# Luna attention and a gated MLP on one core: an earlier load of v2, first scores ahead of the first packed block, and a changed order of fills

## The chip, the cores and the metric

The kernel runs on one core of a Trainium2 chip. The metric is the device time in microseconds of one execution. Before the change the median of 8 runs is 254.1 us (253.71 to 257.84). Instructions are named by engine: PE is TensorE (PEld its weight loads), DVE is VectorE, ACT is ScalarE, POOL is GpSimd, and SP is the queue of SyncE, which only issues DMAs here.

## The reference

```python
def sm_attn(qq, kk, vv):
    s = scale * np.matmul(qq, kk.transpose(0, 1, 3, 2))
    a = softmax(s)                        # max subtracted, sum + 1e-9
    return np.matmul(a, vv)

p_packed = sm_attn(p, k, v)               # p: 32 packed queries a head
out = sm_attn(q, p_packed, p_packed)      # q: 576 queries a head
x = out.transpose(0, 2, 1, 3).reshape(B * S, H * D)
h = x @ w_in                              # 4608 x 512 by 512 x 2048
return (h * np.cos(h)) @ w_out            # 2048 x 512
```

B = 8 batches, H = 8 heads, S = 576 positions, D = 64. The inputs are float32; the kernel computes in bfloat16 with float32 sums.

## The kernel before

The eight batches run one after the other as a software pipeline whose order is written out by hand: each engine executes its own instructions in program order and waits on semaphores for the others.

For one batch b the stages are:

- `load(n, b)` issues on POOL a DMA that casts k, q or v of the batch to bfloat16 (tiles kbf with two buffers, qbf and vbf with one). `permute_v(b)` copies vbf to vp so that heads lie beside each other: 2.75 us on POOL for all batches but the first.
- k and q are transposed, either by TensorE and copies (`pe_T`, batches 0 and 1) or by a DMA issued on SP (`xbar`, from batch 2 on). SP also issues all output DMAs, in program order with these.
- `s1(b)`: scores of the 32 packed queries against k (16 small matmuls, in two halves y, into two PSUM buffers psA), then two exponentials on ACT (tile a1). `recips(b)` makes 1/sum (r1, and rs1 scaled) on DVE from the sums.
- a1 is transposed to a1T by TensorE (`a1_pe`, `a1_one`) or by a DMA on SP (`a1_xbar`).
- `pp(b)`: the packed block, 24 matmuls of vp and a1T; the result is copied to ppT by DVE and ACT.
- `ppw(b, n)`: the packed block times a quarter n of w_in, evacuated to PPW. x is never formed: h is a2n times PPW.
- `s2(b)`: scores of the 576 queries against the packed keys, exponentials (a2u) on ACT. `sums2(b, y)` sums them by a matmul with ones and takes the logarithm on ACT; `normalise(b)` takes two exponentials on ACT and two products on DVE (a2n).
- `h_mm(b, fc)`, fc from 0 to 15: four matmuls give 128 rows of h in a psA buffer, ACT takes the sine with a shift (cosT), DVE multiplies it by the same buffer (gT) and so frees it.
- The output of batch b, 16 matmuls for each chunk of 128 rows, isn't a stage of its own: `fill(n)` issues the next n of these matmuls of the previous batch, and is put where TensorE would wait. A finished chunk is copied to osb by DVE or ACT in turn and sent off by SP. Batch 0 is filled from the end of its own h loop on. The rows 512 to 575 of two batches are joined in one chunk (`joint`, copied by POOL).

`slot(s, hooks, keep, heavy)` runs the 16 steps of h_mm with the fills that are left spread over the steps by weight 1 + heavy[fc]. A hook (fc, f) runs f after step fc; where fc is in heavy, half of the step's fills go ahead of it.

PSUM: pool A has three buffers psA of two banks, taken in turn by everything but the output and the calls with own=True, which take the two banks of pool O.

The change touches `s1` (L133), `a1_one` (L164), the start (L382 to L396), the stretch between batch 0's h loop and slot 1 (L432 to L450), the weights of slots 1 and 2 (L449, L483), and the fills of the loop over batches 3 to 7 (L496, L512). A copy of one element to `gate` on POOL (L444, L479, L504) makes everything behind it on POOL, loads above all, wait until the tile it reads has arrived.

Of the kernel before, what the change touches and what calls it, by code (L numbers as in the profile page):

```python
# [15 lines left out]
def kernel(  # L16
# [55 lines left out]
    def copy(eng, out, in_):  # L72
        if eng is ACT:
            ACT.copy(out=out, in_=in_)  # L74
        else:
            eng.tensor_copy(out=out, in_=in_)  # L76
# [4 lines left out]
    def load(n, b):  # L81
        bf[n, b] = bf_pool.tile([TP, H, C * D], BF16, name=n + "bf", tag=n + "bf", bufs=2 if n == "k" else 1)
        G.dma_start(out=bf[n, b], in_=srcs[n][b].rearrange("h (p c) d -> p h (c d)", c=C))

    def permute_v(b, eng=G):
        vp[b] = vp_pool.tile([TP, C, H * D], BF16, name="vp", tag="vp")
        copy(eng, vp[b].rearrange("p c (h d) -> p c h d", h=H),
             bf["v", b].rearrange("p h (c d) -> p c h d", c=C))
# [5 lines left out]
    def pe_T(n, b, engs=(V, V, V), groups=(0, 1, 2), own=False):  # L94
        if 0 in groups:
            xT[n, b] = att_pool.tile([128, H * 3, TP], BF16, name=n + "T", tag=n + "T", bufs=2 if n == "k" else 1)
        t = xT[n, b]
        flat = bf[n, b].rearrange("p h x -> p (h x)")
        for i in groups:
            ps = bank(BF16) if own else psa(BF16)[:, 0, :]  # L100
            for j in range(8):
                o = 8 * i + j
                nc.tensor.transpose(ps[:, j * TP:(j + 1) * TP], flat[:, o * 128:(o + 1) * 128],  # L103
                                    ident[0:TP, 0:TP])
            copy(engs[i], t[:, 8 * i:8 * i + 8].rearrange("p a x -> p (a x)"),
                 ps[:, 0:8 * TP])

    def bank(dt=FP32):
        return O.tile([128, 512 if dt == FP32 else 1024], dt, name="ot", tag="ot")

    def pack_p(b0, b1, flat=None):
        ng = 2 * (b1 - b0)
        if flat is None:
            flat = psa(BF16).rearrange("p a x -> p (a x)")
        for g in range(ng):
            nc.tensor.transpose(flat[:, g * 128:(g + 1) * 128],
                                p_bf[:, 2 * b0 + g].rearrange("p t d -> p (t d)"), ident)
        V.tensor_copy(out=P2[:, b0:b1].rearrange("p b h n -> p (b h n)"), in_=flat[:, 0:ng * 128])
# [11 lines left out]
            ps.append(t)  # L130
        return ps

    def s1(b):  # L133
        ps = scores(P2[:, b], xT["k", b])
        sm = small.tile([128, 2], FP32, name="sums1")
        for y in range(2):
            ACT.activation(  # L137
                out=a1[b % 2][:, y, :, 0:TP].rearrange("p (e m) x -> p e m x", e=2),
                in_=ps[y][:, :, 0:HS].rearrange("p e (m x) -> p e m x", m=3),
                func=AF.Exp, scale=scale, accum_out=sm[:, y:y + 1])  # L140
        sums1[b] = sm

    def recips(b):
        r1[b] = small.tile([128, 2], FP32, name="r1")
# [19 lines left out]
    def a1_one(b):  # L164
        t = a1T[b] = att_pool.tile([128, 2, C, 128], BF16, name="a1T", tag="a1T")
        ps = psa(BF16)
        for y in range(2):
            for c in range(C):
                nc.tensor.transpose(ps[0:TP, y, c * 128:(c + 1) * 128], a1[b % 2][:, y, c, 0:TP], ident)
            copy(V, t[0:TP, y].rearrange("p c x -> p (c x)"), ps[0:TP, y, 0:C * 128])  # L170

    def pp(b, own=False, engs=(V, ACT)):
# [16 lines left out]
    def ppw(b, n, eng=None, own=False, later=False, cuts=((0, 512),)):  # L189
        if b not in PPW:  # L190
            PPW[b] = ppw_pool.tile([128, 2, DF], BF16, name="PPW", tag="PPW")
        two = isinstance(eng, tuple)
        if own:
            ps = [bank(), bank()]
        else:
            t = psa()
            ps = [t[:, 0, :], t[:, 1, :]]
        for x in range(4):
            for y in range(2):
                r = slice(64 * y, 64 * y + 64)  # L200
                nc.tensor.matmul(ps[y][32 * x:32 * x + 32, :], ppT[b % 2][r, 2 * x + y, :],  # L201
                                 w_in_bf[r, x, n * 512:(n + 1) * 512], start=True, stop=True)

        def evacuate(cuts=cuts):
            if own or two:
                for a, z in cuts:
                    for y in range(2):
                        copy(eng[y] if two else eng, PPW[b][:, y, n * 512 + a:n * 512 + z], ps[y][:, a:z])
            else:
                copy(eng or (V, ACT)[n % 2], PPW[b][:, :, n * 512:(n + 1) * 512], t)  # L210
        if later:
            return [lambda c=c: evacuate((c,)) for c in cuts]
        evacuate()
# [8 lines left out]
    def sums2(b, y):  # L222
        if b not in lns:
            lns[b] = att_pool.tile([128, 2, S], FP32, name="lns", tag="lns")
        ps = psa()
        for e in range(2):
            nc.tensor.matmul(ps[:, e, 0:HS], ones_blk, a2u[b][:, y, e * HS:(e + 1) * HS],  # L227
                             start=True, stop=True)
        ACT.activation(out=lns[b][:, y].rearrange("p (e x) -> p e x", e=2),  # L229
                       in_=ps[:, :, 0:HS], func=AF.Ln)  # L230

    def normalise(b):
        a2n[b] = a2n_pool.tile([128, 2, S], BF16, name="a2n", tag="a2n")
        for y in range(2):
            ACT.activation(out=lns[b][:, y], in_=lns[b][:, y], func=AF.Exp, scale=-1.0)  # L235
        for y in range(2):
            V.scalar_tensor_tensor(out=a2n[b][:, y], in0=a2u[b][:, y], scalar=r1[b][:, y:y + 1],  # L237
                                   in1=lns[b][:, y], op0=ALU.mult, op1=ALU.mult)
# [81 lines left out]
    def fill(n):  # L320
        while n > 0 and filler[1] > 0:
            next(filler[0])
            filler[1] -= 1
            n -= 1
# [13 lines left out]
    def warm(n):  # L338
        wps = bank()
        for _ in range(n):  # L340
            nc.tensor.matmul(wps, wz[:, 0:128], wz, start=True, stop=True)  # L341
# [40 lines left out]
    dup_p(2, 4, V)  # L382
    sums2(0, 0)
    sums2(0, 1)
    pe_T("k", 1, (V, V, V))
    pack_p(1, 2, bank(BF16))
    warm(2)
    cut_ppw, rest_ppw = ppw(0, 0, V, own=True, later=True, cuts=((0, 128), (128, 512)))
    normalise(0)
    cut_ppw()  # L390
    s1(1)
    a1_one(1)
    rest_ppw()
    recips(1)
    load("k", 2)
    permute_v(1)  # L396
    for fc in range(NFC):
        h_mm(0, fc)()
        if fc in (1, 5, 8):
            ppw(0, 1 + fc // 4, (ACT, V), own=True)  # L400
        if fc == 10:
            pp(1, own=True, engs=(ACT, ACT))
        if fc in (11, 12, 13):
            pe_T("q", 1, (V, ACT, V), (fc - 11,), own=True)
        if fc == 13:
            set_filler(0)
        if fc >= 14:
            fill(2)
# [15 lines left out]
    def pw2(b, n=0, eng=None):  # L424
        ppw(b, n, eng)
        ppw(b, n + 1, eng)

    def tk(n, b, i):
# [1 line left out]

    ACT.preload_act_table_set(EXP_SET)
    s2(1)  # L432
    ppw(1, 0, V)
    load("q", 2)
    load("k", 3)
    load("v", 2)
    dup_p(4, 2 * B, G)
    fill(8)
    sums2(1, 0)
    sums2(1, 1)  # L440
    xbar("k", 2)
    xbar("q", 2)
    xbar("k", 3)
    G.tensor_copy(out=gate, in_=xT["k", 3][0:1, 0, 0:1])  # L444
    load("q", 3)
    ppw(1, 1, V)
    normalise(1)
    fill(14)
    slot(1, [(3, lambda: pw2(1, 2, (ACT, V))), (6, lambda: pack_p(2, 5)), (8, lambda: pack_p(5, B)),  # L449
             (8, lambda: (permute_v(2), load("v", 3), load("k", 4)))], 4)  # L450

    fill(1000)
    set_filler(1)
# [26 lines left out]
    for n, b in (("v", 4), ("q", 4), ("k", 5)):  # L480
        load(n, b)
    fill(8)
    slot(2, [(3, lambda: pw2(2, 2, (ACT, V))), (7, lambda: pp(3, engs=(ACT, ACT))), (11, lambda: pw2(3))], 5, {11: 3})  # L483

    for s in range(3, B):
        nxt = s + 1 < B
        fill(1000)
        set_filler(s - 1)
        ACT.preload_act_table_set(EXP_SET)  # L489
        if nxt:  # L490
            permute_v(s + 1)
        s2(s)
        ppw(s, 2, V)
        if nxt:
            xbar("q", s + 1)
        fill(8)  # L496
        if nxt:
            s1(s + 1)
            ppw(s, 3, V)
            a1_xbar(s + 1)  # L500
            recips(s + 1)
            if s + 2 < B:
                xbar("k", s + 2)
                G.tensor_copy(out=gate, in_=xT["k", s + 2][0:1, 0, 0:1])  # L504
        else:
            ppw(s, 3, V)
        fill(4)
        sums2(s, 0)
        fill(5)
        sums2(s, 1)  # L510
        normalise(s)
        fill(13)  # L512
        for n, b in (("v", s + 2), ("q", s + 2), ("k", s + 3)):
            if b < B:
                load(n, b)
        slot(s, [(5, lambda: pp(s + 1, engs=(ACT, ACT))), (10, lambda: pw2(s + 1))] if nxt else [], 5, {10: 3})
# [33 lines left out]
```

The softmax here doesn't subtract the row's maximum and nothing guards it: scores larger than these inputs give would overflow.

## Time and profile before

| | us |
|---|---|
| median of 8 runs | 254.1 |
| profiled execution, device time | 253.97 |
| its span, first to last instruction | 252.2 |
| PE busy | 236.4 |
| ACT busy | 170.7 |
| DVE busy | 162.6 |
| POOL busy | 58.5 |
| mean granted clock of TensorE | 0.998 |

| stretch of the span, us | what runs there | PE busy |
|---|---|---|
| 0 to 17 | start: loads of batch 0, its packed block, its scores | 14.04 of 17 |
| 17 to 40 | batch 1's packed scores, batch 0's h loop | 18.22 of 23 |
| 40 to 64 | batch 1: s2, slot 1 | 23.72 of 24 |
| 64 to 79 | batches 2 and 3: packed scores; s2(2) | 12.98 of 15 |
| 79 to 98 | slot 2 | 18.54 of 19 |
| 98 to 204 | batches 3 to 6 | 104.80 of 106 |
| 204 to 252 | batch 7 and its output | 44.12 of 48 |

Landing times of DMAs that matter (issue to landing, us of the span): w_in's fourth part 12.42 to 30.57, q1 15.31 to 33.25, k2 27.84 to 48.78, q2 40.36 to 51.32, k3 41.12 to 54.59, v2 41.88 to 58.80; the transposes kT2 48.88 to 61.66, qT2 55.69 to 63.55, kT3 61.57 to 66.54; q3 67.13 to 75.59, v3 71.50 to 81.28, k4 72.26 to 84.86; a1T(3) 72.75 to 85.40.

A line of a timeline gives the start and the duration in us, engine, line and operation, what it writes and reads, the count of merged instructions, and in brackets the idle time of the engine before it with what ended it. A line of operations recorded in a helper has the helper's number: L76 is any copy on DVE or POOL, L74 any copy on ACT. Starts of matmuls are recorded, their ends are modelled, so two lines of PE can overlap.

### The profile page before, as it was taken

The page shows a single profiled execution, that of the slowest core. Times are in us where ns is not written, and L with a number is a line of the kernel's source. Part 1 is how long each engine was busy: PE and PEld are TensorE (multiplying, and loading weights), DVE is VectorE, ACT ScalarE, POOL GpSimd, SP SyncE. Part 2 cuts the span into 40 slices and gives each one's busy share as a digit, 9 for nine tenths or more (in the row PEclk, how much of TensorE's full clock was granted, in tenths as well). Part 3 has the DMA queues.
Part 4 walks back from the last instruction along what each step waited for, and adds up shares of the span by engine and source line. Part 5 has one row for each costly group of instructions (what it writes and reads, how often), then busy time and mean ns, then how long its engine had stood idle before and what let it go on. Part 6 is the DMA issues. An engine that isn't in the chain of part 4 may idle for free.

```text
span 252.2 us, 5022 instructions
## 1 busy us (share of the span) xinstructions
PE 236.4 (94%) x2014; PEld 130.8 (52%) x2014; DVE 162.6 (64%) x245; ACT 170.7 (68%) x285; POOL 58.5 (23%) x71
## 2 busy tenths in 40 slices
PE   8886889999969999999999999999999999999993
PEld 3453463566435554465446553565356554665452
DVE  2548986789376977477847675579556874876110
ACT  2366888866558787888886667887877585873000
POOL 8442604200361344104312205020500000000000
PEclk9999999999999999999999999999999999999999
DMA  6999999999999989998999995979461112112133
GB/s 92 202 211 205 205 206 227 199 186 154 187 214 172 188 167 213 218 216 133 218 194 200 155 211 101 180 144 187 99 141 44 42 44 72 36 33 63 48 83 83
DMA packets 65270, 37.67 MB, mean 149 GB/s; under 512 B 37872, under 2 KB 60656, under 8 KB 65248
## 3 DMA queue, kind: packets, MB, share of 16 engines
q0 software_dynamic: 23184, 18.81, 49.2%
q1 hardware_dynamic: 41904, 18.42, 36.9%
q8 instruction: 15, 0.25, 0.4%
q10 hardware_dynamic: 160, 0.13, 0.2%
q14 instruction: 7, 0.06, 0.1%
HBM read 37.22 MB, written 9.44 MB: 185 GB/s over the span
## 4 chain that ended last, share of the span: by engine, by line
PE 76%; ACT 8%; DVE 8%; DMA 4%; issue 2%; POOL 1%; DVEq 0%; POOLq 0%; ACTq 0%
PE ot L303 44%; PE psA L250 21%; DVE gT L257 4%; DMA qbf<-in_q_dram 4%; PE psA L201 3%; ACT cosT L254 2%; PE psA L177 2%; ACT a2u L219 2%; PE psA L227 1%; PE ot L289 1%; PE psA L128 1%; ACT L489 1%; DVE osb L76 1%; DVE rs L147 1%; DVE PPW L76 1%
## 5 line engine op out<-in xcount | busy, mean ns | idle before, releaser
L303 PE MATMUL ot<-w_out_bf,gT 128*128 128x512 bf16 x512 | 132.6, 379 | 0.0
L257 DVE TENSOR_TENSOR gT<-psA,cosT 128x576 bf16<-128x576 f32 x128 | 94.1, 754 | 31.2 <-ACT cosT L254 30.0
L254 ACT ACTIVATE cosT<-psA 128x576 bf16<-128x576 f32 x128 | 82.7, 653 | 29.7 <-PE psA L250 28.0
L250 PE MATMUL psA<-a2n,PPW 128*128 128x288 bf16 x512 | 83.9, 286 | 1.9 <-DVE PPW L76 1.0
L303 PEld LDWEIGHTS <-gT 128*128 128x128 bf16 x512 | 48.0, 98 | 42.6 <-issue 6.1
L250 PEld LDWEIGHTS <-PPW 128*128 128x128 bf16 x512 | 49.1, 98 | 36.5 <-issue 3.8
L76 DVE CAST PPW<-psA 128x1024 bf16<-128x1024 f32 (+1 forms) x23 | 25.8, 1128 | 12.1 <-PE psA L201 12.1
L261 POOL COPY joint<-gT 128x512 bf16<-128x512 bf16 x16 | 9.9, 616 | 86.4 <-DVE gT L257 86.4
L76 DVE COPY osb<-ot 128x512 f32<-128x512 f32 (+1 forms) x19 | 12.8, 671 | 16.9 <-PE ot L303 13.8
L74 ACT COPY osb<-ot 128x512 f32<-128x512 f32 (+1 forms) x18 | 10.3, 572 | 18.7 <-PE ot L303 14.1
L76 POOL COPY vp<-vbf 96x3072 bf16<-96x3072 bf16 x7 | 19.3, 2751 | 2.4 <-DMA vbf<-in_v_dram 2.3
L237 DVE SCALAR_TENSOR_TENSOR a2n<-a2u,r,lns 128x576 bf16<-128x576 bf16 x16 | 12.4, 814 | 9.6 <-ACT lns L235 9.6
L229 ACT ACTIVATE lns<-psA 128x576 f32<-128x576 f32 x16 | 10.3, 652 | 5.7 <-PE psA L227 5.2
L137 ACT ACTIVATE a<-psA 128x576 bf16<-128x576 f32 x16 | 10.3, 649 | 5.0 <-PE psA L128 5.0
L303 PE MATMUL ot<-w_out_bf,joint 128*128 128x512 bf16 x48 | 12.8, 379 | 0.0
L201 PE MATMUL psA<-w_in_bf,ppT 64*32 64x512 bf16 x224 | 10.4, 381 | 1.5 <-DVE gT L257 1.1
L219 ACT ACTIVATE a2u<-psA,rs 128x576 bf16<-128x576 f32 x16 | 11.0, 737 | 1.2 <-PE psA L128 1.0
L254 ACT ACT_TABLE_LOAD x8 | 10.3, 1283 | 0.1
L74 ACT CAST ppT<-psA 64x128 bf16<-64x128 f32 x24 | 6.2, 260 | 5.8 <-PE psA L103 2.9
L235 ACT ACTIVATE lns<-lns 128x576 f32<-128x576 f32 x16 | 10.0, 679 | 0.0
L341 PE MATMUL ot<-wz 128*128 128x512 bf16 x26 | 8.6, 470 | 1.2 <-DVE wz L353 1.2
L74 ACT CAST PPW<-psA 128x1024 bf16<-128x1024 f32 (+1 forms) x9 | 7.2, 825 | 2.6 <-PE psA L201 2.6
(71 smaller groups left out, 143.4 us busy)
## 6 DMA issues: line engine op xcount, KB each, us to landing
kbf<-in_k_dram POOLq DMA_DIRECT2D x8, 576.0 KB, 12.4
vbf<-in_v_dram POOLq DMA_DIRECT2D x8, 576.0 KB, 7.6
qbf<-in_q_dram POOLq DMA_DIRECT2D x8, 576.0 KB, 9.6
out_dram<-osb SPq DMA_DIRECT2D x24, 192.0 KB, 2.6
out_dram<-osb SPq DMA_DIRECT2D x22, 128.0 KB, 2.4
w_in_bf<-in_moe_w_in_dram POOLq DMA_DIRECT2D x4, 512.0 KB, 16.4
w_out_bf<-in_moe_w_out_dram POOLq DMA_DIRECT2D x4, 512.0 KB, 21.1
out_dram<-osb SPq DMA_DIRECT2D x26, 64.0 KB, 2.0
```

Of the source, the lines that this page charges most:

```text
L74: ACT.copy(out=out, in_=in_)
L76: eng.tensor_copy(out=out, in_=in_)
L137: ACT.activation(out=a1[b % 2][:, y, :, 0:TP].rearrange("p (e m) x -> p e m x", e=2), in_=ps[y][:, :, 0:HS].rearrange("p e (m x) -> p e m ...
L201: nc.tensor.matmul(ps[y][32 * x:32 * x + 32, :], ppT[b % 2][r, 2 * x + y, :], w_in_bf[r, x, n * 512:(n + 1) * 512], start=True, stop=True)
L219: ACT.activation(out=a2u[b][:, y].rearrange("p (e x) -> p e x", e=2), in_=ps[y][:, :, 0:HS], func=AF.Exp, scale=rs1[b][:, y:y + 1])
L229: ACT.activation(out=lns[b][:, y].rearrange("p (e x) -> p e x", e=2), in_=ps[:, :, 0:HS], func=AF.Ln)
L235: ACT.activation(out=lns[b][:, y], in_=lns[b][:, y], func=AF.Exp, scale=-1.0)
L237: V.scalar_tensor_tensor(out=a2n[b][:, y], in0=a2u[b][:, y], scalar=r1[b][:, y:y + 1], in1=lns[b][:, y], op0=ALU.mult, op1=ALU.mult)
L250: nc.tensor.matmul(ps[:, e, 0:HS], PPW[b][:, y, fc * 128:(fc + 1) * 128], a2n[b][:, y, e * HS:(e + 1) * HS], start=(y == 0), stop=(y == 1))
L254: ACT.activation(out=csv, in_=ps[:, :, 0:HS], func=AF.Sin, bias=PI_HALF)
L257: V.tensor_tensor(out=gT[b][:, fc, :].rearrange("p (e x) -> p e x", e=2), in0=ps[:, :, 0:HS], in1=csv, op=ALU.mult)
L303: nc.tensor.matmul(pss[c], w, w_out_bf[:, fc, :], start=(fc == 0), stop=(fc == NFC - 1))
```

## The change

`s1` can hand back its exponentials to be called later, so that its matmuls are issued earlier than they are. In `a1_one` all twelve transposes are issued ahead of both copies. In the start, `pack_p(1, 2)` goes ahead of `pe_T("k", 1)`, and the scores of batch 1 ahead of the first `ppw`. `load("v", 2)` moves from behind the loads of q2 and k3 to just behind `permute_v(1)`, and `permute_v(2)` from a hook of slot 1 to ahead of the first gate. `ppw(1, 0)` goes between two groups of fills, nine instead of eight in all. Slots 1 and 2 give step 3 a weight of 4. In batches 3 to 7, two fills move from behind `normalise` to ahead of the next batch's `s1`.

```diff
-    def s1(b):
+    def s1(b, later=False):
         ps = scores(P2[:, b], xT["k", b])
-        sm = small.tile([128, 2], FP32, name="sums1")
-        for y in range(2):
-            ACT.activation(... func=AF.Exp, scale=scale, accum_out=sm[:, y:y + 1])
-        sums1[b] = sm
+        sm = sums1[b] = small.tile([128, 2], FP32, name="sums1")
+
+        def exps():
+            for y in range(2):
+                ACT.activation(... func=AF.Exp, scale=scale, accum_out=sm[:, y:y + 1])
+        if later:
+            return exps
+        exps()
...
     def a1_one(b):
...
         for y in range(2):
             for c in range(C):
                 nc.tensor.transpose(ps[0:TP, y, c * 128:(c + 1) * 128], a1[b % 2][:, y, c, 0:TP], ident)
+        for y in range(2):
             copy(V, t[0:TP, y].rearrange("p c x -> p (c x)"), ps[0:TP, y, 0:C * 128])
...
+    pack_p(1, 2, bank(BF16))
     pe_T("k", 1, (V, V, V))
-    pack_p(1, 2, bank(BF16))
     warm(2)
+    s1_mm = s1(1, later=True)
     cut_ppw, rest_ppw = ppw(0, 0, V, own=True, later=True, cuts=((0, 128), (128, 512)))
     normalise(0)
+    s1_mm()
     cut_ppw()
-    s1(1)
     a1_one(1)
     rest_ppw()
     recips(1)
     load("k", 2)
     permute_v(1)
+    load("v", 2)
...
     s2(1)
-    ppw(1, 0, V)
     load("q", 2)
     load("k", 3)
-    load("v", 2)
     dup_p(4, 2 * B, G)
-    fill(8)
+    fill(4)
+    ppw(1, 0, V)
+    fill(5)
     sums2(1, 0)
     sums2(1, 1)
     xbar("k", 2)
     xbar("q", 2)
     xbar("k", 3)
+    permute_v(2)
     G.tensor_copy(out=gate, in_=xT["k", 3][0:1, 0, 0:1])
...
     slot(1, [(3, lambda: pw2(1, 2, (ACT, V))), (6, lambda: pack_p(2, 5)), (8, lambda: pack_p(5, B)),
-             (8, lambda: (permute_v(2), load("v", 3), load("k", 4)))], 4)
+             (8, lambda: (load("v", 3), load("k", 4)))], 4, {3: 3})
...
-    slot(2, [(3, ...), (7, ...), (11, lambda: pw2(3))], 5, {11: 3})
+    slot(2, [(3, ...), (7, ...), (11, lambda: pw2(3))], 5, {3: 3, 11: 3})
...
     for s in range(3, B):
...
-        fill(8)
+        fill(10)
         if nxt:
             s1(s + 1)
...
         normalise(s)
-        fill(13)
+        fill(11)
```

More of the change, by code (lines that the diff above doesn't have):

```diff
@@ L131, in scores @@
         return ps
-    def s1(b):
+    def s1(b, later=False):
         ps = scores(P2[:, b], xT["k", b])
-        sm = small.tile([128, 2], FP32, name="sums1")
-        for y in range(2):
[L137 to L140, printed above, removed]
-        sums1[b] = sm
+        sm = sums1[b] = small.tile([128, 2], FP32, name="sums1")
+        def exps():
+            for y in range(2):
+                ACT.activation(
+                    out=a1[b % 2][:, y, :, 0:TP].rearrange("p (e m) x -> p e m x", e=2),
+                    in_=ps[y][:, :, 0:HS].rearrange("p e (m x) -> p e m x", m=3),
+                    func=AF.Exp, scale=scale, accum_out=sm[:, y:y + 1])
+        if later:
+            return exps
+        exps()
     def recips(b):
@@ L482 @@
     fill(8)
-    slot(2, [(3, lambda: pw2(2, 2, (ACT, V))), (7, lambda: pp(3, engs=(ACT, ACT))), (11, lambda: pw2(3))], 5, {11: 3})
+    slot(2, [(3, lambda: pw2(2, 2, (ACT, V))), (7, lambda: pp(3, engs=(ACT, ACT))), (11, lambda: pw2(3))], 5, {3: 3, 11: 3})
     for s in range(3, B):
```

## The prediction

> **What bounds the kernel now.** I read first the busy shares, the 40 slices and the chain of waits, then the idle stretches of TensorE one by one in the timeline, then when each load landed.
>
> ```profile
> PE 236.4 (94%) x2014; PEld 130.8 (52%) x2014; DVE 162.6 (64%) x245; ACT 170.7 (68%) x285; POOL 58.5 (23%) x71
> PE   8886889999969999999999999999999999999993
> DMA  6999999999999989998999995979461112112133
> PE 76%; ACT 8%; DVE 8%; DMA 4%; issue 2%; POOL 1%; DVEq 0%; POOLq 0%; ACTq 0%
> ```
>
> TensorE is the bound: 94% busy, 76% of the chain, granted clock 0.998. So a change pays where it takes away TensorE idle time that isn't given back later. The digits show where that is: the first 40 us, one slice near 69 us (the 6), little after. The DMA row warns that the engines are full for two thirds of the span. The recorded idle gaps sum to 10.6 us; as ends of matmuls are modelled, I price a wait by start-to-start intervals against a place where the same pair runs without a wait. These are the waits that the change touches:
>
> ```profile
> 21.32 0.54 PE L169 MATMUL psA<-ident,a 128*96 128x128 bf16 x6 [0.73 <-ACT a L137]
> 22.50 0.49 PE L169 MATMUL psA<-ident,a 128*96 128x128 bf16 x6 [0.64 <-DVE a1T L76]
> 24.11 0.88 PE L250 MATMUL psA<-a2n,PPW 128*128 128x288 bf16 x4 [0.62 <-DVE PPW L76]
> ...
> 39.79 0.41 PE L201 MATMUL psA<-w_in_bf,ppT 64*32 64x512 bf16 x8 [0.61 <-DVE gT L257]
> ...
> 49.94 0.41 PE L201 MATMUL psA<-w_in_bf,ppT 64*32 64x512 bf16 x8 [0.25 <-DVE gT L257]
> ...
> 68.45 2.75 POOL L76 COPY vp<-vbf 96x3072 bf16<-96x3072 bf16 x1
> 69.02 2.21 DVE L147 TENSOR_SCALAR rs<-r 128x2 f32<-128x2 f32 x1
> 71.26 0.87 PE L177 MATMUL psA<-a1T,vp 96*128 96x64 bf16 x24 [1.92 <-DVE rs L147]
> ...
> 83.03 0.41 PE L201 MATMUL psA<-w_in_bf,ppT 64*32 64x512 bf16 x8 [0.27 <-DVE gT L257]
> ...
> 131.94 0.75 PE L250 MATMUL psA<-a2n,PPW 128*128 128x288 bf16 x4
> ...
> 154.93 0.44 PE L128 MATMUL psA<-kT,P 64*32 64x288 bf16 x16 [0.31 <-ACT a2u L219]
> ```
>
> The largest is the 1.92 us before batch 2's packed block. The profile names DVE's rs, but that product doesn't read rs: it reads vp, and POOL's permute of v2 ends at 71.20, 0.06 before it.
>
> [...] L147 takes 0.17 us elsewhere and 2.21 under that permute, ending with it. [...] the transpose a1T(3), issued while q3, v3 and k4 load, lands after 12.65 us; a later one after 3.9. [...] the wait at 22.50 comes from the order copy-then-transposes, not from a need[...].
>
> **The change part by part.** No computation is added or removed: matmuls, activations, copies and loads keep their counts, and fills that leave one place return in another. Only order moves; the closure `later` and the split loop of a1_one issue nothing.
>
> *A, start (L382-396).* pack_p(1) (0.28 us of PE, 0.28 of DVE) goes ahead of pe_T(k1), whose copies end some 0.3 later, at 20.0 instead of 19.69. But the scores then wait for neither P (19.61+0.28) nor ppw(0,0): they end at about 20.35, the first exponential starts near 20.2 instead of 20.53, the second half's transposes near 21.6 instead of 22.50. What ends last is now DVE: a2n 1.54, PPW cut 0.48, two a1T copies 1.10, rest 1.01, from 20.0 on: rest is done at 23.95, was 24.52. That is 0.5. Not all survives: ppw(0,3) reads the fourth w_in, landed 30.57, and ran at 30.92; pe_T(q1) ran at 33.58, q1 landed at 33.25. I take -0.4 (0.0 to -0.6).
>
> *B, v2 (L396, L436, L450).* load(v2) moves on POOL's queue to just after permute_v(1), which ends at 31.37. POOL's loads run eight deep (issue 12 waited for landing 4, issue 17 for 9); v2, now the 18th, needs the tenth, landed 30.57, so its 0.77 us of issue don't wait; the joint copy behind it, at 31.90, slips 0.25 and is read at 93. It follows k2 (landed 48.78) and lands near 51.4, a load's spacing of 2.5 later; permute_v(2), behind dup_p (ends 47.78), then runs 51.4 to 54.2 instead of 68.45. The gate behind it waits until 66.6 anyway. pp(2) then waits only for scores: from 68.90 + 0.25 it starts about 2.1 sooner (start-to-start 2.20 after the last score, 0.1 unhindered). Next late would be s2(2), waiting for ACT's ppT casts behind a1's exponentials, ending 70.66 + 0.65: 0.05. So -2.05. Also v3 and k4 leave at 68.5 and 69.3 instead of 71.50 and 72.26, since no permute stands ahead of them.
>
> *C, ppw(1,0) behind four fills (L433).* It waits for gT's product until 39.74; 4 x 0.216 us cover that: -0.8 of start-to-start excess. Sums2's second half then waits for a2u's end at 41.63, some 0.2 back: -0.6.
>
> *D, weight {3: 3} in slots 1 and 2.* Three fills (0.65) between h_mm(3) and the two ppw cover DVE's lag. Excess at 49.27-50.88 against the unhindered pair at 92: about 0.6; at 82.36-83.96: 0.8. Other steps get 1.5 to 1.7 fills instead of 1.7 to 2.1: 0.49 + 1.5 x 0.216 = 0.81 us a step against DVE's 0.76, still enough. -0.55 and -0.75.
>
> *E, two fills from after normalise to before s1 (slots 3 to 7).* Before: sums2's second half at T, then 13 fills, the third matmul of h_mm(0) at T + 3.05 + 0.245. Its a2n is ready at T + 3.25: (slot 3: 103.40, 105.13 + 1.54; slot 5: 158.10, 159.80 + 1.55; slot 4, T + 3.34, already stretches the group to 0.75 from 0.65.) The cover is exactly used up. With 11 fills TensorE arrives 0.43 sooner relative to T and waits 0.39. In slots 5 and 6 the two fills fill the wait on a2u (0.31 + 0.19 of gap), T stays, and the gain ahead is the loss behind: 0. In 3, 4 and 7 nothing waited there: T is 0.43 later and 0.39 is lost each. +1.15.
>
> *DMA remainder.* TensorE would reach pp(4) near 107.4 (111.32 - 4.35 + 0.39). Its a1T(4), landed 110.25, stands on SP behind the transpose of q4, which waited for q4's landing (101.73), and that chain goes back over the gate on kT4 to k4's landing (84.86). v3 and k4 leave 3 us sooner, but q3 (67.13 to 75.59) doesn't, so I give the chain 2 to 3 us: +0.5 (0 to +1.1).
>
> Sum: -0.4 - 2.05 - 0.6 - 0.55 - 0.75 + 1.15 + 0.5 = **-2.7 us**. The profiled execution took 253.97 (span 252.2, 1.8 around it), so 251.3; the median of the eight runs is 0.13 above it: **251.4**.
>
> **The rivals.**
> *E costs nothing* (the h_mm wait isn't there, or two fills were worth it): -3.85, 250.2. For: waits in slots 5 and 6 are real. Against: the a2n times above.
> *The transfers don't come sooner*: a1T(3) lands at 85.4 again while pp(3), three fills later in its slot, is reached at 87.21 - 4.35 + 0.65 = 83.5: 1.9 us given back, in place of the 0.5: -1.3; if v2's permute is held as well, as when the load or the gate keeps its old time, B's gain goes too and it is 253 to 254. For: a full DMA row. This includes that the change doesn't do what it says.
> *Slower: the swap starves k3.* v2 ahead of q2 and k3 moves k3 from third to last in the stream, 54.59 to 58.80. SP issues its transpose at 61.57 anyway, 2.8 after that, and the same three loads lie in the stream, so I expect kT3 at 66.5 again. If instead the 4.2 us pass through whole, kT3 lands at 70.7, s1(3), reached near 67.3, loses 3.4 and the sum is +0.7; with q2's delay added in series (8.4) it is +5: 254.8 to 259. It decides from kT3 about 3.5 us late on.
>
> **How the numbers follow.** About 1% (2.5 us) is what a measurement of this kernel tells from no change. Main case 0.50 (250.4 to 252.2, two thirds beyond -1%); E free 0.20, all beyond; transfers late 0.20, within; starved k3 0.10, two thirds beyond +1%. The bar lies at 251.56. Faster 0.33 + 0.20 and a little, 0.55; slower 0.07; same 0.38. Range 249.8 to 253.6: main, E free and most of the late case.
>
> **What would show it.** A: no wait for DVE between the a1 transposes, first cosine near 22.9 (23.52). B: the permute of v2 near 51 to 54, L147 at 0.17, pp(2) within 0.2 of the scores. C, D: no gap at the moved ppw. E: the first h_mm group of slots 3 to 7 stretched from 0.65 to about 1.05. DMA: kT3 still near 66.5; a1T(3) before pp(3). The prediction is wrong if kT2 or kT3 lands later than TensorE asks, or if TensorE waits for a1T(3) or a1T(4) longer than 1 us.

## The result, and the profile after

The kernel with the change takes **257.41 us** (median of 11 runs, 255.79 to 260.5), the kernel before 254.18 (32 runs, 253.35 to 257.84): a ratio of 1.0107, with a 95% interval of 1.0081 to 1.0132. It is slower by some 3 us. Medians here are of all runs, ratios of the undisturbed ones alone: now and then one of these kernels runs 1 to 2% slower (the one after 260.5 us in one run, at a granted clock of 0.983). The profiled execution took 257.41 as well, with a span of 255.4 at a granted clock of 0.993, against 252.2 before.

First the page of the kernel after: its busy times, three rows of the 40 slices, and the shares of the chain that ended last.

```profile
PE 239.1 (94%) x2014; PEld 131.0 (51%) x2014; DVE 163.8 (64%) x245; ACT 170.8 (67%) x285; POOL 58.5 (23%) x71
...
PE   8887889999999899959999999999999999999993
...
PEclk9999999999999999979999999999999999999999
DMA  6999999999899989996999993979371112111133
...
PE 67%; DMA 11%; DVE 9%; ACT 9%; issue 2%; POOL 1%; DVEq 0%; POOLq 0%; ACTq 0%
```

The 6 near 69 us is gone from the PE row: the gap that the change went for is closed. A 5 stands further on instead, in the slice 108.5 to 114.9, and in the clock's row a 7 in the same place. TensorE's share of the chain fell from 76% to 67%, and that of the DMAs rose from 4% to 11%. The work is the same (each engine has as many instructions as before). TensorE's busy time grew by 2.7 us, in part because some of it ran at a lower clock (0.50 from 112.07 to 115.48 us).

The timeline of the kernel after, in the places that the prediction named:

```profile
20.79 1.17 PE L173 MATMUL psA<-ident,a 128*96 128x128 bf16 x12 [0.49 <-ACT a L139]
...
50.93 2.75 POOL L76 COPY vp<-vbf 96x3072 bf16<-96x3072 bf16 x1 [3.67 <-DMA vbf<-in_v_dram]
...
67.44 0.44 PE L128 MATMUL psA<-kT,P 64*32 64x288 bf16 x16
...
67.81 0.87 PE L182 MATMUL psA<-a1T,vp 96*128 96x64 bf16 x24
...
84.99 0.86 PE L182 MATMUL psA<-a1T,vp 96*128 96x64 bf16 x24 [0.94 <-DMA a1T<-a]
...
104.59 0.41 PE L255 MATMUL psA<-a2n,PPW 128*128 128x288 bf16 x2 [0.30 <-DVE a2n L242]
...
112.19 1.44 PE L182 MATMUL psA<-a1T,vp 96*128 96x64 bf16 x24 [3.02 <-DMA a1T<-a]
```

The twelve transposes of a1(1) run as one row, with no copy between. v2's permute runs at 50.93, and pp(2) (67.81) follows the scores at once, where it waited 1.92 us. Then come two waits that the kernel before hadn't: pp(3) waits 0.94 us and pp(4) 3.02 us for the DMA transpose of a1. pp(4), the packed block of batch 4, also takes 1.44 us, where 0.86 is usual.

How the lead came and went is read from the start of s2(b) on TensorE, the same instructions in both traces:

| | before, us | after, us | after - before |
|---|---|---|---|
| s2(2) | 73.36 | 69.92 | -3.44 |
| s2(3) | 98.20 | 95.51 | -2.69 |
| pp(4) | 111.32 | 112.19 | +0.87 |
| s2(4) | 123.69 | 126.08 | +2.39 |
| s2(5) | 152.13 | 154.93 | +2.80 |
| s2(6) | 178.16 | 180.96 | +2.80 |
| s2(7) | 207.27 | 210.07 | +2.80 |
| end of the span | 252.2 | 255.4 | +3.2 |

Whatever TensorE gains ahead of pp(4) ends there, because pp(4) starts when a1T(4) lands, and a1T(4) lands 1.8 us *later* than before (112.05 against 110.25). From pp(4) on the account is short: +0.87 of pp(4)'s start, +1.52 between pp(4) and s2(4) (13.89 us against 12.37), +0.4 in each of slots 4 and 7: 3.2.

The stretches behind pp(4)'s wait, before and then after. The columns are the window, its length, busy time and instructions of PE, PEld, DVE, ACT and POOL, then the granted clock, the DMA share and GB/s:

```profile
106.00:112.00 6.00, 5.93 (x58) 3.89 (x57) 4.68 (x7) 4.88 (x7) 0.00 (x0) 1.00 1.15 222
112.00:117.00 5.00, 5.00 (x46) 2.99 (x45) 3.66 (x5) 4.11 (x9) 2.63 (x5) 1.00 0.74 148
```

```profile
106.00:112.00 6.00, 3.11 (x21) 1.82 (x19) 4.55 (x7) 2.99 (x5) 0.00 (x0) 1.00 1.12 181
112.00:117.00 5.00, 4.81 (x42) 3.31 (x43) 0.81 (x2) 2.34 (x6) 0.18 (x1) 0.66 0.86 184
```

After the wait TensorE is busy again, 4.81 of 5 us, but at a mean clock of 0.66. In finer windows the clock is at half, 0.50, from 112.07 to 115.48 us and full on both sides: the wait is paid for, and then more.

And the queue of SP from 70 to 113 us, after and then before: start, time that the issue took, line and transfer.

```profile
70.65 5.40 SPq L155 DMA_TRANSPOSE a1T<-a  x1
76.16 8.54 SPq L92 DMA_TRANSPOSE qT<-qbf  x1
...
104.20 3.65 SPq L92 DMA_TRANSPOSE qT<-qbf  x1
107.94 1.47 SPq L155 DMA_TRANSPOSE a1T<-a  x1
```

```profile
72.75 6.05 SPq L151 DMA_TRANSPOSE a1T<-a  x1
...
101.78 4.43 SPq L92 DMA_TRANSPOSE qT<-qbf  x1
106.31 1.47 SPq L151 DMA_TRANSPOSE a1T<-a  x1
```

a1T(3) is issued 2.1 us sooner (70.65) and lands 0.54 us sooner (84.86, was 85.40). a1T(4) stands behind the transpose of q4, which waits for q4 (landed 104.15, was 101.73), as the prediction had it; but that chain hasn't come forward by 2 to 3 us, it has gone back by 2.4.

| landing, us | before | after |
|---|---|---|
| v3, k4 (issued 71.50 and 72.26; after 68.02 and 68.78) | 81.28, 84.86 | 80.74, 84.67 |
| kT3, kT4 | 66.54, 90.75 | 66.11, 90.73 |
| v4, q4, k5 (issued from 91.8 on in both) | 98.91, 101.73, 106.16 | 100.20, 104.15, 107.02 |
| a1T(3), a1T(4) | 85.40, 110.25 | 84.86, 112.05 |

**The theory to test** (T, and L in the later expectations): the loads and transposes of batches 3 to 5 run in a loop of their own. The gate on kT(s+1) lets the next loads go; the transposes on SP come through only when those loads have landed; kT(s+2) needs the transposes. The loop's times (kT3 66.5, kT4 90.7) don't depend on when TensorE is ready, so a lead of TensorE becomes a wait for a1T. The rivals: the two moved fills of E cost the time (F), v2's earlier load makes the later transfers late (V), or the mere order on SP is what costs. Part names A to E are those of the prediction.

### The profile page after: what moved, and what is told of

The parts are those of the page before. It is cut to its first block, busy times and chain, and to the rows that moved or that the text cites. A ratio compares the mean times of both kernels' runs of the same rounds, so it can differ in the third digit from the quotient of the medians.

```text
span 255.4 us, 5023 instructions
## 1 busy us (share of the span) xinstructions
PE 239.1 (94%) x2014; PEld 131.0 (51%) x2014; DVE 163.8 (64%) x245; ACT 170.8 (67%) x285; POOL 58.5 (23%) x71
## 4 chain that ended last, share of the span: by engine, by line
PE 67%; DMA 11%; DVE 9%; ACT 9%; issue 2%; POOL 1%; DVEq 0%; POOLq 0%; ACTq 0%
PE ot L308 36%; PE psA L255 20%; DMA a1T<-a 7%; DMA qbf<-in_q_dram 4%; DVE a2n L242 3%; PE psA L206 3%; DVE gT L262 2%; PE psA L182 2%; PE psA L128 2%; ACT a2u L224 2%; ACT cosT L259 2%; PE ot L294 1%; PE psA L232 1%; DVE PPW L76 1%; DVE rs L151 1%
## 5 line engine op out<-in xcount | busy, mean ns | idle before, releaser
L255 PE MATMUL psA<-a2n,PPW 128*128 128x288 bf16 x512 | 85.2, 287 | 3.7 <-DVE PPW L76 1.5
L76 DVE COPY osb<-ot 128x512 f32<-128x512 f32 (+1 forms) x19 | 12.8, 671 | 16.0 <-PE ot L308 12.7
L76 POOL COPY vp<-vbf 96x3072 bf16<-96x3072 bf16 x7 | 19.3, 2750 | 12.7 <-DMA vbf<-in_v_dram 8.6
L182 PE MATMUL psA<-a1T,vp 96*128 96x64 bf16 x168 | 6.6, 200 | 4.2 <-DMA a1T<-a 4.0
```

Source lines behind the costliest of these rows:

```text
L182: nc.tensor.matmul(ps[:, hp * 64:(hp + 1) * 64], vp[b][:, c, hp * 128:(hp + 1) * 128], a1T[b][0:TP, :, j, 32 * hp:32 * hp + 32], start=(j ...
L255: nc.tensor.matmul(ps[:, e, 0:HS], PPW[b][:, y, fc * 128:(fc + 1) * 128], a2n[b][:, y, e * HS:(e + 1) * HS], start=(y == 0), stop=(y == 1))
```

## The experiments

Ratios are to the kernel before on the same chip, with their 95% intervals. The kernel before took 254.51 us in the runs of experiments 1 to 4, 254.43 in 5 to 8 and 254.88 in 9 to 12.

### 1. Part E alone, in the kernel before

```diff
-        fill(8)
+        fill(10)
         if nxt:
             s1(s + 1)
...
-        fill(13)
+        fill(11)
```

> The kernel before with step E alone (10 and 11 fills instead of 8 and 13 in batches 3 to 7). Theory T, transfers: what made the change slower is that TensorE gets ahead of the DMAs, and waits for a1T(3) and above all a1T(4), 3.0 us in the profile of the changed kernel, with a lowered clock after it. E alone then costs only what was predicted for it, 0.39 us in each of slots 3, 4 and 7: +1.15 us, ratio about 1.0045, first h_mm groups stretched to about 1.05 us, no wait for a1T over 0.5 us. Rival F, fills: E is the main loss, +3 us or more, ratio 1.012 or more. Rival that E is free: ratio 1.000 or less.

Measured: 255.47 us, 1.0034 (1.0010 to 1.0058). Against the kernel before, taking off a difference of 0.47 us that stands at s2(3) already, ahead of every moved fill, slots 3 to 7 cost +0.40, +0.40, 0, 0 and +0.38 of the span: 1.2 us, as predicted (1.15). The timeline of slot 4 shows how:

```profile
131.96 1.55 DVE L237 SCALAR_TENSOR_TENSOR a2n<-a2u,r,lns 128x576 bf16<-128x576 bf16 x2 [2.33 <-ACT lns L235]
...
133.56 0.41 PE L250 MATMUL psA<-a2n,PPW 128*128 128x288 bf16 x2 [0.30 <-DVE a2n L237]
```

With two fills fewer behind normalise, TensorE comes to the second half of the first h group before DVE has written the second half of a2n (131.96 + 1.55 = 133.51). E explains at most 1.2 of the 3.2 us, and nothing of the wait at pp(4).

### 2. The change without part E

The reverse edit in the kernel after: `fill(10)` to `fill(8)`, `fill(11)` to `fill(13)`.

> The changed kernel with step E undone (8 and 13 fills again). Theory T: the wait before pp(4) ends when a1T(4) lands, so slot 3's part returns nothing, and only slots 4 and 7 give 0.39 each: -0.8 us against the changed kernel, that is still +2 to +2.5 us, ratio about 1.009; the wait for a1T(4) is 0.3 to 0.4 us longer. Rival F: back to or below the kernel before, ratio 1.000 or less.

Measured: 257.41 us, 1.0101 (1.0062 to 1.0139): no better than the whole change, where 0.8 us less was expected. The timeline shows the packed block of batch 4:

```profile
112.97 1.44 PE L182 MATMUL psA<-a1T,vp 96*128 96x64 bf16 x24 [3.47 <-DMA a1T<-a]
```

The wait is longer, 3.47 us instead of 3.02, a1T(4) lands at 112.84, and the clock is at half for twice as long, from 111.87 to 118.69 us; pp(4) to s2(4) takes 15.09 us. In this execution, what E's absence saves later is lost in a longer wait and a longer spell of half clock. The fills don't explain the loss.

### 3. a1's transpose ahead of q's on SP

In the kernel after, for batches 3 to 6:

```diff
         ppw(s, 2, V)
-        if nxt:
-            xbar("q", s + 1)
         fill(10)
...
             a1_xbar(s + 1)
+            xbar("q", s + 1)
             recips(s + 1)
```

> The changed kernel with one order on SP changed: in batches 3 to 6 the transpose of a1 is issued ahead of the transpose of the next q, so that it doesn't stand behind q's load. Theory T: a1T(4) is issued near 101 instead of 107.94 and lands before pp(4) asks for it near 108.9, the 3.0 us wait and the low clock after it go: -3 to -4 us against the changed kernel, 253.0 to 254.3 us, ratio 0.996 to 1.001. If the wait is owed to full DMA engines alone and not to the order on SP, a1T(4) lands as late as before and the time stays at 1.010 or so.

Measured: 253.81 us, 0.9953 (0.9932 to 0.9974), 3.6 us less than the change alone. SP's queue, then TensorE's timeline around pp(4):

```profile
100.14 3.51 SPq L155 DMA_TRANSPOSE a1T<-a  x1
103.76 4.79 SPq L92 DMA_TRANSPOSE qT<-qbf  x1
```

```profile
109.03 0.86 PE L182 MATMUL psA<-a1T,vp 96*128 96x64 bf16 x24
```

a1T(4) is issued at 100.14 and lands at 108.62; pp(4) runs at 109.03 without a wait and in 0.86 us, and the mean clock of the span is 1.000. Issued 7.8 us sooner it lands only 3.4 sooner: k5, the last of the loads, landed at 107.50. That is enough: the change's own gain appears once pp(4) doesn't wait.

### 4. Part B alone, in the kernel before

`load("v", 2)` behind `permute_v(1)`, and `permute_v(2)` ahead of the gate, nothing else of the change.

> The kernel before with step B alone (v2 loaded ahead of q2 and k3, its permute ahead of the gate). Theory T: pp(2) starts about 2.0 us sooner, then TensorE reaches pp(4) near 109.3 while a1T(4) lands between 110.3 and 112: 1 to 2.7 us go back, ratio 0.998 to 1.004. Rival V, that the load order itself does the harm by making k3, kT3 and all behind them late: kT3 lands 2 us or more after 66.5 and the ratio is 1.008 or more. Rival that nothing comes back: -2 us, ratio 0.992.

Measured: 256.94 us, 1.0046 (0.9986 to 1.0106). s2(2) comes 1.98 us sooner, net of 0.47 at the start, where -2.05 was predicted. The timeline at pp(4):

```profile
112.83 1.44 PE L177 MATMUL psA<-a1T,vp 96*128 96x64 bf16 x24 [2.65 <-DMA a1T<-a]
```

The lead of one part suffices for the wait and the clock (at half from 112.41 to 115.82 us). The time fits this but doesn't show it: it rests on few runs, its interval includes 1, and it lies just above what T allowed (1.004). k3 landed 4.6 us later than before (59.23), yet kT3 at 66.87 against 66.54: SP issues k3's transpose only at 61.93, behind two others, and so V falls in the form given, that kT3 comes late.

### 5. Control: the order of experiment 3 in the kernel before

> A control: the kernel before with the order on SP of e3 alone (a1's transpose ahead of the next q's). Theory T: the kernel before doesn't wait for a1T(4) (pp(4) is reached 1.1 us after it landed), so the order has nothing to take away: ratio 0.998 to 1.001. Rival O, that the order on SP is worth 1 us or more by itself and e3 tells nothing of the change: ratio 0.996 or less.

Measured: 254.24 us, 0.9987 (0.9967 to 1.0007). The order on SP is worth nothing by itself, as the kernel before doesn't wait at pp(4). So the 3.6 us of experiment 3 are the change's lead let through, with the clock kept up, not a second improvement.

### 6. The order of experiment 3, without part E

> The changed kernel with step E undone and a1's transpose first on SP. Theory T: with the wait for a1T(4) gone, E's price shows in full, so undoing it gives 0.9 to 1.2 us against e3, where e2 gave nothing: 252.2 to 253.0 us, ratio 0.990 to 0.993 to the kernel before. Rival: E costs nothing once the wait is gone, ratio 0.995 as in e3.

Measured: 252.89 us, 0.9924 (0.9902 to 0.9946), against 253.81 with E. That is 0.9 us less in the medians, which fits E's price, but the two ratios' intervals overlap, so it isn't shown. Nor is the wait gone in this trace. pp(3) still waits 1.26 us and pp(4) 1.41: a1T(3) landed at 85.22, and a1T(4), behind k5 (110.01), at 110.84.

### 7. As 6, with pp(3) behind step 9 of slot 2

The hook `(7, pp(3))` becomes `(9, pp(3))`.

> As e6, with pp(3) behind step 9 of slot 2 instead of step 7. Theory T: a1T(3) lands near 84.9 whatever TensorE does, and pp(3), reached near 84.3, waits 0.6 us; two steps later it is reached near 86 and waits for nothing: -0.5 us against e6, ratio 0.988 to 0.991. It could cost if ppT, copied by ACT, isn't ready for pw2(3) behind step 11.

Measured: 251.80 us, 0.9875 (0.9836 to 0.9913), over six runs. Only its times are read here, so that pp(3)'s wait going away is not shown for this kernel; experiment 11 shows it.

### 8. q4 loaded ahead of v4

```diff
-    for n, b in (("v", 4), ("q", 4), ("k", 5)):
+    for n, b in (("q", 4), ("v", 4), ("k", 5)):
```

> The changed kernel, order on SP as it was, with q4 loaded ahead of v4 in front of slot 2. Theory T, that pp(4) waits because a1T(4) stands on SP behind q4's landing: q4 lands near 100 instead of 104.15, a1T(4) is issued near 104.5 and lands near 108.5, the 3.0 us wait falls below 0.5 us and the time to 254.0 to 255.0, ratio 0.999 to 1.002. If only the sum of the transfers counts, a1T(4) lands near 112 again and the ratio stays near 1.011.

Measured: 256.59 us, 1.0080 (1.0047 to 1.0113): the expectation is missed. q4 landed at 100.54, 3.6 us sooner, as expected, but SP then took 6.39 us to issue its transpose; a1T(4) was issued at 107.08 and landed at 111.68, and pp(4)'s wait stayed (3.45 us from start to start). So it isn't q4's landing that sets a1T(4)'s. The table gathers when a1T(4) was issued and landed, beside the landing of k5, the last of the three loads:

| kernel | a1T(4) on SP | issued | k5 landed | a1T(4) landed | between |
|---|---|---|---|---|---|
| before | behind q4's | 106.31 | 106.16 | 110.25 | 4.1 |
| after | behind q4's | 107.94 | 107.02 | 112.05 | 5.0 |
| 8 (q4 ahead of v4) | behind q4's | 107.08 | 107.71 | 111.68 | 4.0 |
| 3 (change, a1 first) | first | 100.14 | 107.50 | 108.62 | 1.1 |
| 5 (before, a1 first) | first | 102.17 | 106.17 | 107.73 | 1.6 |
| 6 (no E, a1 first) | first | 100.07 | 110.01 | 110.84 | 0.8 |

A transpose that is first on SP lands 0.8 to 1.6 us after the last load, though it was issued 4 to 10 us ahead of it. One behind q4's is issued only when SP is done with issuing that, within 1 us of k5's landing in all three, and then takes 3.9 to 4.6 us. This corrects T: in these traces not q4's landing, but loads still under way hold the transposes, the first one in its transfer, the second by holding SP.

### 9. Parts A, C and D alone

The kernel after with B and E undone.

> The changed kernel with B and E undone, so A, C and D alone; v2 is loaded and permuted where it was. Theory L, a loop of transfers: from kT3 on, loads wait for a gate, transposes wait until the loads are through, and the next gate waits for the transposes, so a1T(3) and a1T(4) land at fixed times and any lead of TensorE over about 1 us is taken back at pp(4). A, C and D give a lead of about 2.0 us there (start to pp(3) about 1.5, slot 2's weight 0.75); pp(4) is reached near 109.3, a1T(4) lands near 111 to 112.5, and with or without a lowered clock after it the ratio is 0.998 to 1.008. Rival V, that loading v2 early is what spoils the transfers: no wait over 0.5 us, ratio 0.991 to 0.994.

Measured: 255.09 us, 0.9989 (0.9951 to 1.0027): no gain from three parts that the prediction put at -2.3 us together. But the lead was taken back elsewhere than expected. Its timeline near 69 us:

```profile
67.52 0.18 POOL L451 COPY gate<-kT 1x1 bf16<-1x1 bf16 x1 [18.81 <-DMA kT<-kbf]
...
68.78 3.37 DVE L151 TENSOR_SCALAR rs<-r 128x2 f32<-128x2 f32 x1
...
69.38 2.75 POOL L76 COPY vp<-vbf 96x3072 bf16<-96x3072 bf16 x1
...
72.18 1.46 PE L182 MATMUL psA<-a1T,vp 96*128 96x64 bf16 x24 [3.08 <-DVE rs L151]
```

Here v2's permute stands behind the gate on kT3, so pp(2) can't run before 69.38 + 2.75 = 72.13, however early TensorE is: the same kind of take-back, 3.08 us of idle time, at another time of the loop. The clock follows here too: it is at half from 71.75 to 75.16 us. pp(4) then doesn't wait (113.11; a1T(4) landed at 110.90, where 111 to 112.5 was expected). In the full change B takes that permute out from behind the gate.

### 10. k4's load held until a1T(3) has landed

```diff
-             (8, lambda: (load("v", 3), load("k", 4)))], 4, {3: 3})
+             (8, lambda: load("v", 3))], 4, {3: 3})
...
     recips(3)
+    G.tensor_copy(out=gate, in_=a1T[3][0:1, 0, 0, 0:1])
+    load("k", 4)
```

> The changed kernel with k4's load held by a gate until a1T(3) has landed. Theory L: a1T(3) lands about 1 us after the last load issued before it, now v3: near 81 instead of 84.9, and pp(3)'s wait of 1.1 us goes. k4 lands near 88 to 89, kT4 and the loads behind it 2 to 4 us later, a1T(4) near 114 to 116, and pp(4) waits 5 us or more: slower than the changed kernel, ratio 1.014 to 1.025. If transposes are slow of themselves, a1T(3) lands near 84 as before.

Measured: 258.50 us, 1.0173 (1.0108 to 1.0238). The timeline of POOL:

```profile
81.15 0.18 POOL L474 COPY gate<-a1T 1x1 bf16<-1x1 bf16 x1 [11.01 <-DMA a1T<-a]
...
82.60 2.74 POOL L76 COPY vp<-vbf 96x3072 bf16<-96x3072 bf16 x1
```

With one load fewer in the stream a1T(3) landed at 81.03 instead of 84.86, 0.93 after v3, now the last load (80.10). Loads do hold the transpose, shown on the transfer itself. As a version it is worse: v3's permute stands behind the gate on POOL and pp(3) waits 1.57 us for it, and k4 (87.95), kT4 (92.80) and a1T(4) (113.91) all come later: a delay put into the loop travels round it. But pp(4) waits only 1.45 us, not the 5 expected: TensorE comes late itself. v4's permute (102.70 to 105.45) now meets a2n on DVE, whose two products take 3.53 us instead of 1.55, TensorE waits 1.77 us for the first, and the clock is at half from 107.88 to 111.29. So the time was forecast rightly in part by luck.

### 11. As 7, with pp(s + 1) behind step 7 in batches 3 to 6

> As e7 (no fills moved, a1 first on SP, pp(3) behind step 9 of slot 2), with pp(s + 1) behind step 7 instead of 5 in batches 3 to 6. Theory L: it gives the transposes 1.6 us more, so what is left of the wait for a1T(4) (0 to 1.4 us in e3 and e6) goes: ratio 0.985 to 0.990, no wait over 0.3 us for a1T. If ppT isn't ready for pw2 behind step 10, it is slower than e7.

Measured: 251.46 us, 0.9884 (0.9830 to 0.9938), over six runs; in the profile (span 249.5) neither pp(3) (86.65) nor pp(4) (110.32) waits for a1T. It isn't told apart from 7. Both beat the kernel before by some 1.2% and the changed one by more than 2%.

### 12. The wait kept, TensorE kept busy in it

In the kernel after, twelve more matmuls on zeros stand ahead of pp(4); their result isn't used. They add work and take none away.

```diff
+            if s == 3:
+                wps = psa()[:, 0, :]
+                for _ in range(12):
+                    nc.tensor.matmul(wps, wz[:, 0:128], wz, start=True, stop=True)
             pp(s + 1, engs=(ACT, ACT))
```

> The changed kernel with 12 extra matmuls of zeros (2.6 us) ahead of pp(4) alone, where TensorE waits 3.0 us anyway; their result is not used. It tells apart the wait and the clock after it: if 1.5 us of the loss are owed to the clock (0.66 granted from 112 to 117, pp(4) to s2(4) 13.9 us instead of 12.4), the clock stays at 1.00, that stretch takes 12.4 us and the time is 1 to 1.5 us less than the changed kernel's: ratio 1.004 to 1.007. If the slow matmuls behind the wait have another cause, nothing changes: 1.010.

Measured: 255.99 us, 1.0050 (1.0027 to 1.0073), some 1.4 us less than the changed kernel, for matmuls that compute nothing. Its timeline and windows, columns as above:

```profile
109.13 2.75 PE L528 MATMUL psA<-wz 128*128 128x512 bf16 x12
...
111.71 0.87 PE L182 MATMUL psA<-a1T,vp 96*128 96x64 bf16 x24
```

```profile
106.00:112.00 6.00, 5.71 (x42) 3.32 (x42) 4.50 (x7) 2.94 (x5) 0.00 (x0) 1.00 1.15 209
112.00:117.00 5.00, 4.95 (x49) 3.34 (x47) 2.57 (x4) 3.71 (x9) 1.45 (x3) 1.00 0.62 144
```

The clock stays at 1.00, pp(4) takes 0.87 us again, and pp(4) to s2(4) 12.38 us, as before the change (12.37). The runs agree: the mean clock of the span is 0.996 or more in all of the 22 but one, while in the kernel after it is 0.993 or less in all but one, which is its fastest (255.79 us). So of the loss about 1.5 us are the clock and not the wait.

## Why the prediction was wrong

It said 251.4 us (249.8 to 253.6) and gave slower 0.07; measured were 257.41. Its account of TensorE's own work was right nearly throughout; one step, on the transfers, failed. It had named the sign itself: it would be wrong if TensorE waited for a1T(3) or a1T(4) longer than 1 us.

- **A, C, D in slot 1, and B:** predicted together -3.6 us at s2(2), measured -3.44 (-3.26 without the 0.18 by which this execution is ahead at s2(0), before any part has acted). The transposes of a1(1) run unbroken and the first cosine starts at 22.68 (predicted near 22.9); v2's permute runs at 50.93 (51.4); pp(2) starts 0.22 us after the last score, from start to start. The product rs (L147, now L151) was put at 0.17 us there and took 1.22, beside a small copy and two load issues on POOL (67.47 to 68.79), but nothing waits for it. Alone, B gave -1.98 (predicted -2.05).
- **D in slot 2:** the gap ahead of the ppw is gone, predicted -0.75. From s2(2) to s2(3) the kernel lost 0.75 us net, with 1.11 us of start-to-start wait at pp(3) in it, so D gave about 0.4 there, half of the forecast, if the difference is D's alone.
- **E:** right in size and in place: +1.15 predicted, 1.2 in experiment 1, 0.4 in slots 3, 4 and 7 and none in 5 and 6. The rival "E costs nothing" is false. In the changed kernel slot 3's share lies ahead of pp(4), where the landing sets the time, so only 0.8 of it is paid.
- **The starved k3:** k3 landed at 58.54 (58.80 predicted) and kT3 at 66.11; the prediction had it at 66.5 again, and the slower rival is false. Slower came about by another way.
- **The DMA remainder is the step that failed:** "v3 and k4 leave 3 us sooner, but q3 … doesn't, so I give the chain 2 to 3 us: +0.5 (0 to +1.1)". v3 and k4 did leave 3.5 us sooner, and landed 0.5 and 0.2 sooner; kT4, the gate of the next round, landed at 90.73 instead of 90.75. The chain moved by nothing up to kT4, and then back. The trace of before had the reason in view: v3 and k4 took 9.8 and 12.6 us from issue to landing in a full stream; issued 3.5 us sooner they took 12.7 and 15.9, so that the earlier issue wasn't an earlier end. Nor is q4's landing, to which the prediction traced a1T(4), what sets it (experiment 8). The rival "The transfers don't come sooner" had this and worked it out for pp(3) alone (1.9 us given back; 1.11 measured), not for pp(4), which TensorE now reached 2.1 us sooner than before, to wait 3.31 us from start to start (0.30 before).
- **Two terms were missing.** a1T(4) landed 1.8 us later than before. q4 and k5 landed 2.4 and 0.9 later, though they were issued at the same time (why is left open below), and at pp(4) the lead isn't merely used up (0), but turned into +0.87. And a wait was priced at its length; this one also took the clock down to half for 3.4 us, another 1.52. With the 0.8 of E that makes the 3.2.

How the loads and the transposes share the DMA engines can be read by queue. These are the loads' queue (q0) and SP's (q1) of the kernel after from 77 to 83 us, with v3, k4, a1T(3) and q3's transpose under way: packets, MB, and share of the DMA engines' time.

```profile
q0 software_dynamic: 1121, 0.85, 90.3%
q1 hardware_dynamic: 1122, 0.29, 36.9%
```

As many packets of each pass, but those of SP's queue are a third as large, so it gets a quarter of the bytes and 187 packets a microsecond; from 87 to 90 us, with no load about, it gets 938. Ahead of that, from 70 to 75 us, only 62 of 1039 packets are under 512 bytes, as all of SP's are from 87 to 90, where it moves kT4's transpose: the rest of SP's 318 is output sent off before a1T(3). So a1T(3), issued at 70.65, lands at 84.86, just behind the last load (84.67).

**Left open:** why q4 lands some 2 us later than before at the same issue time. Experiment 1, which has no lead ahead of slot 3, has it as well (103.92), experiment 4, with B alone, too (104.44), and experiments 5 and 9 haven't (101.5 to 102.2). So whether B's order of loads has a part in it isn't decided. That the output chunks go out at other times, and so take other places in the stream, is a guess; it wasn't tried, and the traces don't bear it out alone: of the chunks issued from 91.5 us on, two had landed by q4's landing in the kernel after and one in that before, but one in experiment 1 as well. Experiment 8 shows only that q4's landing alone doesn't decide. Nor is it shown that the loop stays fixed for later batches; from batch 5 on no packed block waits for its transpose.

## What to carry to other kernels

Before counting a saving in TensorE's waits, go forward to the next instruction that waits for a transfer, and ask what sets that transfer's time: if it is a loop of loads, gates and transposes in a full stream, the lead ends there, and it pays only together with an edit that takes the transfer out of the way (here the order of two transposes, worth nothing by itself and 3.6 us with the change). Put the transfer that the bounding engine needs first ahead on its queue, and move its reader later where other work is at hand. And a wait of TensorE can cost more than its length: with the half clock behind it, 1.5 us more for one of 3.02 us (the kernel after) and 2.7 for one of 3.47 (experiment 2), but nothing more for one of 3.16 (experiment 8).

## What the runs showed of the hardware

**A wait that costs more than its length.** In the five traces of the table in which the clock falls ahead of the end of the span, it is at half for 3.41 us, in experiment 2 for twice that (111.87 to 118.69). In the kernel after it is at half from 112.07 to 115.48, then full for 139.95 us, 41 times 3.413, to 255.43. So the traces are laid out here in stretches of 3.41 us, and beside each stands how much of it TensorE was idle:

| kernel | stretch at full clock, us | TensorE idle in it, us | clock in the next |
|---|---|---|---|
| after | 108.66 to 112.07 | 2.90 | 0.50 |
| 9 | 68.33 to 71.75 | 2.65 | 0.50 |
| 2 | 108.45 to 111.87 | 2.42 | 0.50 |
| 4 | 108.99 to 112.41 | 2.28 | 0.50 |
| 10 | 104.46 to 107.88 | 1.96 | 0.50 |
| 8 | 107.01 to 110.42 | 1.83 | 1.00 |
| 8 | 110.42 to 113.83 | 1.39 | 1.00 |

Half clock follows the five stretches with 1.96 to 2.90 us of idle time, and not the two of experiment 8 with 1.83 and 1.39. The traces of before and after, laid out so from 6.3 us on, have three stretches with more than 1.46 us: that of the table, 247.69 to 251.10 before (2.93) and 252.02 to 255.43 after (3.41). Half clock follows each of them, and none of the others. Experiment 8's wait of 3.16 us is longer than the kernel after's 3.02, but its clock stays full (mean 1.000) and pp(4) to s2(4) at 12.36 us. That this is because the wait falls across two stretches is an estimate from these rows; no run moved a wait against them.

**A small instruction that ends with a large copy.** In experiment 9 the product rs, 128 x 2 values and 0.17 us at 74.53, took 3.37 us at 68.78 and ended within 0.02 us of POOL's permute (72.15 and 72.13), as in the kernel before (2.21 us, 71.23 and 71.20). In the kernel after the timeline shows the pair at v4's permute:

```profile
100.32 2.75 POOL L76 COPY vp<-vbf 96x3072 bf16<-96x3072 bf16 x1 [4.10 <-PE psA L232]
...
100.42 2.67 DVE L151 TENSOR_SCALAR rs<-r 128x2 f32<-128x2 f32 x1
```

v4 landed at 100.20, and its permute ran beside rs on DVE: they end at 103.07 and 103.09. In experiment 9 the profile names rs as what pp(2) waited for, although that product doesn't read it: two instructions that end together have one releaser in the list, and the program says which of them counts.
